# Attention weights transposed as F32R from a tile that takes over the slot, and a narrower low half in the product with V

## The chip, the cores and the metric

The kernel runs on one core of a Trainium2 chip. The engines are called as in the profile: PE (TensorE, matmuls), PEld (TensorE's weight loads), DVE (VectorE), ACT (ScalarE), POOL (GpSimd), SP (SyncE, which issues the DMAs). The metric is the device time of one execution in microseconds (us), lower is better. The kernel before took 742.23 us, the median of three runs (740.42, 742.23 and 747.87).

## The reference

The computation is an attention with a hash mask, followed by two dense layers of 1536 tokens. Attention has 2 batches of 8 heads, 768 tokens and a head width of 64:

```python
q_bits = (np.einsum('bhsd,dk->bhsk', q, proj) > 0).astype(np.int64)   # k_bits the same way
mask = q_bucket[:, :, :, None] == k_bucket[:, :, None, :]
scores = np.where(mask, scale * np.matmul(q, k.transpose(0, 1, 3, 2)), -1000000000.0)
attn = np.exp(scores - np.max(scores, axis=-1, keepdims=True))
attn = attn / (np.sum(attn, axis=-1, keepdims=True) + 1e-09)
x = np.matmul(attn, v)                       # laid out as 1536 x 512
h = x @ w_in                                 # 512 -> 2048, then an activation
x = (h * np.tanh(softplus(h))) @ w_out       # 2048 -> 512
h = x @ w_in2
out = (h - np.tanh(h)) @ w_out2
```

Everything is float32 in and out.

## The kernel before, in words

All matmuls but the transposes work on F32R, a float32 of reduced precision in the same four bytes. To keep precision, an operand x is split into a high part xh (x copied to F32R) and a low part xl (x - xh), and a product is a sum of the parts' products.

**Attention** goes through eight pairs of heads (`pairs`), and in a pair through two heads and two halves of the 768 queries. One such quarter (a *group* below, 32 in all) has three score tiles of 128 queries by 768 keys (`scores`, tiles `p`): four matmuls (L582, L583), a clamp with the row's minimum on DVE (L586), and the exponential with its row sum on ACT (L609), in place in `p`. Then come six *chunks* of 128 keys (`chunk`, 192 in all). A chunk transposes the three 128x128 blocks of its keys from the three score tiles into one PSUM tile `pt` (L643: three transposes, float32, against the constant identity `ident`), copies `pt` to the high part `ph` on ACT (L659) and takes the low part `pl` on DVE (L662); in three of twelve chunks ACT copies to `f` (L651) and POOL makes both parts (L375, L655). Four chunks later (`PV_LAG`) `product` multiplies the 128 columns of `vt`, V's high half beside its low half, with `ph` (L622) and with `pl` (L623), each 384 columns wide, and adds up over the six chunks in one PSUM tile `o`. `gather` folds the two halves of `o` together (L672 on ACT, L675 on DVE), and `finish` scales by the reciprocal sums. In between, the next pair's `piece` products (L478 to L480, with a stationary of 64 columns) and splits are made, on ACT (L423, L430, L461), DVE and POOL.

**The dense layers** follow at about 235 us and take the rest of the time. Their weights are turned from int64 into float, split and kept by DVE and ACT while PE multiplies.

**The order** on every engine is fixed beforehand by the planner `Plan`: each `op` has an engine, an estimated cost, a priority key and the buffers that it uses, and a list scheduler emits the operations in the order of their planned starts. Each engine then runs its instructions in that order and waits on semaphores. Tiles come from pools with a fixed number of slots per tag (`p` has `P_BUFS` = 6); a tile that takes a slot waits until all work on the slot's former tile is done. What an `op` emits besides its own engine's instructions stands at that place in the other engine's queue, and the planner doesn't know of it.

Of the kernel before, what the change touches and what calls it, by code (L numbers as in the profile page):

```python
# [27 lines left out]
F32 = mybir.dt.float32  # L28
# [19 lines left out]
G_BUFS, E_BUFS, GX_BUFS, F_BUFS = 3, 3, 2, 2  # L48
T_BUFS, P_BUFS, U_BUFS = 4, 6, 3
RAW_BUFS = 5  # L50
# [11 lines left out]
SLOWP = 0.4  # L62
SPARE = 1
LATE = 0.22
LATS = 0.15
# [214 lines left out]
def tile_lsh_attention_moe(  # L280
# [57 lines left out]
    for name, tags, n in (*wd, *wb):  # L338
# [4 lines left out]
    core = (  # L343
        ("stack", "a b c d", 2), ("p", "p", P_BUFS), ("vt", "vt", 3), ("gx", "ph pl", GX_BUFS),
        ("u", "u", U_BUFS), ("r", "r", 2), ("rt", "rt", 2), ("small", "mn mn2 sums", 6),
# [15 lines left out]
    pjh = const.tile([P, 64], F32R, name="pjh")  # L361
    pjl = const.tile([P, 64], F32R, name="pjl")
    rds = [const.tile([P, 32], F32, name=f"rd{i}") for i in range(2)]
    tiny = const.tile([P, 2, TB], F32, name="tiny")
# [200 lines left out]

    def scores(g, h, half, t, key):

# [3 lines left out]
        used = slice(0, NR + D) if g or h else slice(0, P)  # L571
        p, mn = buf("p", "p", [P, S]), buf("small", "mn", [P, 1])
        sm = sums[g, half]
# [28 lines left out]
        else:  # L602
            sc = buf("ps_s", "s", [P, 2, 512])
            flat = lambda: sc().rearrange("p a b -> p (a b)")
            op("PE", 0.69, key, lambda: products([(kc, flat()[:, kc]) for kc in parts]), reads, [sc])
            op("DVE", 0.87, key + 0.1, lambda: clamp(p(), flat()[:, :S], mn()), [sc], [(p, 0), (p, 1), mn])
        op(
            "ACT", 0.93, key + 0.2,
            lambda: nc.scalar.activation(  # L609
                out=p(), in_=p(), func=AF.Exp, bias=mn(), scale=-1.0,  # L610
                accum_out=sm()[:, h, t:t + 1],
            ),
            [mn, (p, 0), (p, 1)], [p, (sm, h, t)],
        )
        return p

    def product(todo, key):

        vt, c, ph, pl, o, done = todo

        def emit():
            nc.tensor.matmul(o()[:, :HB], vt()[:, c, :], ph()[:, :HB], start=(c == 0), stop=False)  # L622
            nc.tensor.matmul(o()[:, :HB], vt()[:, c, :], pl()[:, :HB], start=False, stop=(c == NT - 1))  # L623

        op("PE", 0.35, key, emit, [(vt, 0), (vt, 1), ph, pl], [o])
        if done:
            done()
# [3 lines left out]
    def chunk(g, h, half, c, ps, o, key, done):  # L631
# [8 lines left out]

        def transpose(ts):
            for t in ts:
                nc.tensor.transpose(pt()[:, t * P:(t + 1) * P], ps[t]()[:, c * P:(c + 1) * P], ident)  # L643

        op("PE", 0.327, key, lambda: transpose(range(TB)), ps, [(pt, 0), (pt, 1)])
        if len(queue) >= PV_LAG:
# [83 lines left out]
    for g in range(len(pairs)):  # L730
# [22 lines left out]
        for h in range(2):  # L753
            for half in range(2):
                n = (2 * g + h) * 2 + half
                ps = [
                    scores(g, h, half, t, at(NT * n + 2 * t - AHEAD) + 0.3) for t in range(TB)
                ]
                o = buf("ps_t", "pt", [P, 512])
                if h == 1:  # L760
                    inverse(g, half, at(NT * n - 2))

                def done(g=g, h=h, half=half, o=o, u=us[half], key=at(NT * (n + 1)) + PV_LAG):
                    gather(h, o, u, key)
                    if h == 1:
                        finish(g, half, u, key + 0.3)

                for c in range(NT):
                    chunk(g, h, half, c, ps, o, at(NT * n + c), done if c == NT - 1 else None)
# [645 lines left out]
    nc.vector.tensor_copy(pjh, pj)  # L1415
    nc.vector.tensor_tensor(out=pjl, in0=pj, in1=pjh, op=ALU.subtract)
    for o in plan.order():
        o.fn()
# [57 lines left out]
```

## Time and profile before

| | |
|---|---|
| median of 3 runs | 742.23 us |
| fastest run | 740.42 us |
| span of the profiled execution, first to last instruction | 739.1 us |
| PE busy | 727.7 us, 98% of the span |
| DVE, ACT, POOL busy | 87%, 72%, 24% of the span |
| POOL's work | all of it in the first 240 us |

The profiled execution's own time is not listed apart from the three runs; its span of 739.1 us is 1.3 us below the fastest of them and 3.1 us below the median, so a few microseconds around the span belong to a run's time. A busy time is the union of an engine's instructions, each taken until its result is out. Instructions of one engine overlap there: the next one may start before the last one has ended. So what an engine needs for a stream of instructions is read from the distance of their starts, as the chain of waits shows it, and not from the mean duration of one.

### The profile page before, as it was taken

What the parts mean: (1) busy time and instruction counts of PE and PEld (TensorE: products, weight loads), DVE (VectorE), ACT (ScalarE), POOL (GpSimd) and SP (SyncE); (2) the same over time, 40 slices, a digit from 0 to 9 for tenths busy, and PEclk for the clock granted to TensorE, in tenths of its full rate; (3) what the DMA queues carried; (4) which work ended last, traced back from release to release, by engine and by line L of the source; (5) the groups of instructions that cost most, each with busy time, mean ns of one, the idle gap of its engine ahead of it and who ended that gap; (6) DMA issues with size and microseconds to landing.
All of it is one profiled execution on the core that took longest, in us unless ns stands there. A gap on an engine that the chain in (4) does not pass through costs nothing.

```text
span 739.1 us, 13094 instructions
## 1 busy us (share of the span) xinstructions
PE 727.7 (98%) x4382; PEld 673.6 (91%) x4382; DVE 643.8 (87%) x1372; ACT 529.7 (72%) x1140; POOL 179.7 (24%) x224
## 2 busy tenths in 40 slices
PE   7999999999999999999999999999999999999998
PEld 4889999999999999999999999998998899999997
DVE  6988998998999999999898899789898775767893
ACT  6989999999997866767676676666565445466660
POOL 5677987988961000000000000000000000000000
PEclk9999999999999999999999999999999999999999
DMA  7775775785562655545655567999986786735621
GB/s 215 184 200 130 204 201 129 204 211 126 156 175 88 231 197 168 172 156 179 204 181 186 185 232 247 330 330 329 350 295 251 270 278 232 244 144 186 222 87 64
DMA packets 59390, 150.96 MB, mean 204 GB/s; under 512 B 7990, under 2 KB 20406, under 8 KB 59324
## 3 DMA queue, kind: packets, MB, share of 16 engines
q1 hardware_dynamic: 58892, 149.65, 63.9%
q8 instruction: 34, 0.56, 0.3%
q10 hardware_dynamic: 432, 0.49, 0.2%
q14 instruction: 32, 0.26, 0.1%
HBM read 88.18 MB, written 43.04 MB: 178 GB/s over the span
## 4 chain that ended last, share of the span: by engine, by line
PE 93%; DVE 2%; DMA 2%; ACT 2%; issue 1%; POOL 0%; ACTq 0%; SPq 0%; DVEq 0%; POOLq 0%
PE pt L1023 11%; PE pt L1025 11%; PE pt L1024 11%; PE pt L643 8%; PE pt L1101 6%; PE pt L1113 6%; PE s L1100 6%; PE pt L1100 6%; PE pt L1338 5%; PE s L582 4%; PE pt L622 4%; PE pt L623 4%; PE s L583 4%; PE s L1338 3%; PE s L1113 3%; DVE p L586 1%
## 5 line engine op out<-in xcount | busy, mean ns | idle before, releaser
L1023 PE MATMUL pt<-xh,a 128*128 128x384 f32 x288 | 96.7, 336 | 0.0
L1025 PE MATMUL pt<-xh,a 128*128 128x384 f32 x288 | 96.7, 336 | 0.0
L1024 PE MATMUL pt<-xl,a 128*128 128x384 f32 x288 | 96.6, 335 | 0.0
L586 DVE TENSOR_SCALAR_CACHE_REDUCE p<-s 128x768 f32<-128x768 f32 x93 | 88.2, 948 | 7.6 <-PE s L583 5.7
L609 ACT ACTIVATE p<-p,mn 128x768 f32<-128x768 f32 x96 | 90.7, 945 | 3.1 <-DVE p L586 2.0
L662 DVE TENSOR_TENSOR pl<-pt,ph 128x384 fp32r<-128x384 f32 x148 | 78.5, 546 | 8.6 <-ACT ph L659 7.6
L643 PE MATMUL pt<-cst,p 128*128 128x128 f32 x576 | 83.8, 272 | 1.1 <-DVE pl L662 1.1
L643 PEld LDWEIGHTS pt<-cst,p 128*128 128x128 f32 x576 | 69.5, 140 | 6.1 <-DVE pl L662 1.4
L659 ACT CAST ph<-pt 128x384 fp32r<-128x384 f32 x148 | 68.8, 484 | 5.2 <-PE pt L622 3.1
L1101 PE MATMUL pt<-gh,o 128*128 128x256 f32 x256 | 71.7, 280 | 0.0
L622 PE MATMUL pt<-ph,vt 128*128 128x384 f32 x192 | 70.4, 367 | 0.3 <-ACT f L651 0.2
L582 PE MATMUL s<-b,a 128*128 128x512 f32 (+1 forms) x186 | 68.2, 367 | 1.1 <-DVE p L586 0.7
L623 PE MATMUL pt<-pl,vt 128*128 128x384 f32 x192 | 64.9, 338 | 0.4 <-DVE pl L662 0.4
L583 PE MATMUL s<-d,c 77*128 77x512 f32 (+3 forms) x186 | 59.3, 340 | 0.6 <-ACT raw L846 0.6
L802 DVE TENSOR_TENSOR gl<-pl,gh 128x384 fp32r<-128x384 f32 x96 | 52.4, 551 | 6.5 <-ACT gh L1047 6.5
L1023 PEld LDWEIGHTS pt<-xh,a 128*128 128x128 f32 x288 | 54.1, 188 | 3.3 <-ACT pl L1042 0.2
L1024 PEld LDWEIGHTS pt<-xl,a 128*128 128x128 f32 x288 | 54.1, 188 | 1.3
L1025 PEld LDWEIGHTS pt<-xh,a 128*128 128x128 f32 x288 | 54.1, 188 | 0.1
L1047 ACT CAST gh<-pl 128x384 fp32r<-128x384 f32 x96 | 48.7, 514 | 2.1 <-DVE pl L802 1.1
L1101 PEld LDWEIGHTS pt<-gh,o 128*128 128x128 f32 x256 | 48.3, 189 | 0.0
L1061 ACT COPY ph<-pt 128x384 f32<-128x384 f32 x56 | 26.9, 481 | 28.7 <-PE pt L1025 28.6
L1100 PE MATMUL pt<-gh,o 128*128 128x512 f32 x128 | 47.2, 391 | 0.0
(301 smaller groups left out, 2080.7 us busy)
## 6 DMA issues: line engine op xcount, KB each, us to landing
w<-w SPq DMA_DIRECT2D x52, 512.0 KB
raw<-in_moe_w_in_dram SPq DMA_DIRECT2D x32, 512.0 KB
raw<-in_moe_w_out_dram SPq DMA_DIRECT2D x32, 512.0 KB
split<-a SPq DMA_DIRECT2D x24, 512.0 KB
a<-split SPq DMA_DIRECT2D x24, 512.0 KB
w<-t SPq DMA_DIRECT2D x32, 256.0 KB
o<-split SPq DMA_DIRECT2D x24, 256.0 KB
b<-kh SPq DMA_DIRECT2D x30, 192.0 KB
```

The costliest lines, as they stand in the source:

```text
L582: nc.tensor.matmul(o, a()[:, tok], b_()[:, kc], start=True, stop=False)
L583: nc.tensor.matmul(o, c_()[used, tok], d_()[used, kc], start=False, stop=True)
L586: nc.vector.tensor_scalar(out=out, in0=in_, scalar1=MASKED, scalar2=None, op0=ALU.min, op1=ALU.min, accum_out=low)
L609: lambda: nc.scalar.activation(out=p(), in_=p(), func=AF.Exp, bias=mn(), scale=-1.0, accum_out=sm()[:, h, t:t + 1],),
L622: nc.tensor.matmul(o()[:, :HB], vt()[:, c, :], ph()[:, :HB], start=(c == 0), stop=False)
L623: nc.tensor.matmul(o()[:, :HB], vt()[:, c, :], pl()[:, :HB], start=False, stop=(c == NT - 1))
L643: nc.tensor.transpose(pt()[:, t * P:(t + 1) * P], ps[t]()[:, c * P:(c + 1) * P], ident)
L1023: nc.tensor.matmul(o, tl()[:, 0, c], at_(0, kk), start=start and kk == 0, stop=False, skip_group_check=not start)
L1024: nc.tensor.matmul(o, tl()[:, 0, c], at_(1, kk), start=False, stop=False, skip_group_check=not start)
L1025: nc.tensor.matmul(o, tl()[:, 1, c], at_(0, kk), start=False, stop=kk == 1, skip_group_check=not start)
L1100: nc.tensor.matmul(a()[:, n, :], w()[:, y, c], flat[x][:, :SEG], start=st, stop=sp)
L1101: nc.tensor.matmul(r()[:, 0, rest], w()[:, y, c], flat[x][:, SEG:], start=st and d % 2 == 0, stop=sp, skip_group_check=True)
```

## The change

The three transposes of a chunk are no longer all float32. At a group's first chunk (`c == 0`) one block, that of the third score tile, is transposed as before, in float32. Then each of the three score tiles gets a successor, `p.split`, of the same size and in the same slot, but of type F32R; the slot holds what the exponential left there. POOL clears 8 columns behind the 768 (`PAD`), which makes it the writer of the new tile. All other transposes of the group, two in the first chunk and three in each later one, read `p.split` with an F32R copy of the identity, `idr`. There are 32 float32 transposes left and 544 as F32R. So that one tile's slot can pass on, each of the now 7 `p` buffers has its own tag with one slot. The exponentials of a group are kept in order, and so are the later groups' chunks behind the first (`after`).

In `product`, `pl` meets only the 64 columns of V's high half (the product of the two low halves is left out), and it comes first in all chunks but the first of a group. Three planner costs change: 0.23 for a chunk's transposes (0.327 before), 0.3 for those of a first chunk, 0.34 for a product (0.35 before).

```diff
-T_BUFS, P_BUFS, U_BUFS = 4, 6, 3
+T_BUFS, P_BUFS, U_BUFS = 4, 7, 3
+PAD, PAD_W = 8, 8
+T_COST, T_FIRST, PV_COST = 0.23, 0.3, 0.34
...
+    idr = const.tile([P, P], F32R, name="idr")
...
-        p, mn = buf("p", "p", [P, S]), buf("small", "mn", [P, 1])
+        p, mn = buf("p", f"p{n % P_BUFS}", [P, S + PAD]), buf("small", "mn", [P, 1])
...
+        def high():
+            nc.tensor.matmul(o()[:, :HB], vt()[:, c, :], ph()[:, :HB], start=(c == 0), stop=(c == NT - 1), skip_group_check=True)
+
+        def low():
+            nc.tensor.matmul(o()[:D, :HB], vt()[:, c, :D], pl()[:, :HB], start=False, stop=False, skip_group_check=True)
+
         def emit():
-            nc.tensor.matmul(o()[:, :HB], vt()[:, c, :], ph()[:, :HB], start=(c == 0), stop=False)
-            nc.tensor.matmul(o()[:, :HB], vt()[:, c, :], pl()[:, :HB], start=False, stop=(c == NT - 1))
+            for f in (high, low) if c == 0 else (low, high):
+                f()
...
-        def transpose(ts):
-            for t in ts:
-                nc.tensor.transpose(pt()[:, t * P:(t + 1) * P], ps[t]()[:, c * P:(c + 1) * P], ident)
-
-        op("PE", 0.327, key, lambda: transpose(range(TB)), ps, [(pt, 0), (pt, 1)])
+        def turn(t, src, unit):
+            to = pt()[:, t * P:(t + 1) * P]
+            nc.tensor.transpose(to if unit is ident else to.bitcast(F32R), src[:, c * P:(c + 1) * P], unit)
+
+        def transpose():
+
+            left = list(range(TB))
+            if c == 0:
+                turn(left.pop(), ps[-1](), ident)
+                for p in ps:
+                    p.split = plan.pools["p"].tile([P, S + PAD], F32R, tag=p.tag, name="split")
+                    nc.gpsimd.memset(p.split[:, S:S + PAD_W].bitcast(F32), 0.0)
+            for t in left:
+                turn(t, ps[t].split, idr)
+
+        first = op("PE", T_COST if c else T_FIRST, key, transpose, ps, [(pt, 0), (pt, 1)], after=ps[0].first if c else ())
+        if c == 0:
+            ps[0].first = [first]
...
+    nc.vector.tensor_copy(idr, ident)
```

The planner makes a new order of all engines from this. Three places:

PE before, in the second pair of heads, from the last product ahead of the pair's last group to that group's chunks (`cst` is the identity, `s` and `pt` are PSUM tiles, `vt` is V's halves).

```order
L622 MATMUL pt<-ph,vt 128x384 [waits Activation_49]
L623 MATMUL pt<-pl,vt 128x384 [waits DVE_49]
L643 MATMUL pt<-cst,p 128x128 x2
L643 MATMUL pt<-cst,p 128x128 [waits Activation_49]
L582 MATMUL s<-b,a 128x512 [waits DVE_49]
L583 MATMUL s<-d,c 128x512
L582 MATMUL s<-b,a 128x256
L583 MATMUL s<-d,c 128x256
L643 MATMUL pt<-cst,p 128x128 x6
```

PE after, at the same place of the program.

```order
L652 MATMUL pt<-cst,p_1270 128x128 [waits Activation_49]
L652 MATMUL pt<-idr,split 128x128 x5
L585 MATMUL s<-b,a 128x512 [waits DVE_49]
L586 MATMUL s<-d,c 128x512
L585 MATMUL s<-b,a 128x256
L586 MATMUL s<-d,c 128x256
L652 MATMUL pt<-idr,split 128x128 x3
L628 MATMUL pt<-pl,vt 64x384 [waits Pool_49]
L625 MATMUL pt<-ph,vt 128x384
L652 MATMUL pt<-idr,split 128x128 x3
L628 MATMUL pt<-pl,vt 64x384
L625 MATMUL pt<-ph,vt 128x384
```

The transposes stand in runs of three, six or nine as before (128 runs, 126 before). The F32R ones carry no wait on POOL, which writes only the columns behind the 768. Behind a run stands the 64-column low product in 56 cases and a 64-column `piece` in 8, a 128-column matmul in the other 64.

POOL after, in the third pair of heads, at the first chunk of its last group (L378 copies with a new type, L677 makes a low part).

```order
L562 TENSOR_TENSOR vt<-v,vt 128x6x64 [waits Pool_49]
L661 MEMSET split 128x8
L661 MEMSET split 128x8 [waits Activation_49]
L661 MEMSET split 128x8 [waits PE_49]
L378 TENSOR_SCALAR ph<-f 128x384 [waits Activation_49]
L677 TENSOR_TENSOR pl<-f,ph 128x384 [waits Pool_49]
L378 TENSOR_SCALAR kh<-k 128x384 [waits DMAHW5_49,DMAHW4_49,DMAHW3_49]
```

Each of the 32 groups adds three such clears to POOL's queue, the third behind the wait for the float32 transpose; before, POOL had none of them.

DVE before, in the second pair of heads, around the clamps of the last two score tiles of the group shown for PE (L586 is the clamp that writes a score tile, L662 makes a low part).

```order
L586 TENSOR_SCALAR p,mn<-s 128x768 [waits PE_49]
L695 STREAM_TRANSPOSE rt<-rd_128 128x32 [waits DMAHW6_49,DMAHW7_49,DMAHW0_49,DVE_49]
L662 TENSOR_TENSOR pl<-pt,ph 128x384 [waits Activation_49] x2
L586 TENSOR_SCALAR p,mn<-s 128x768 [waits PE_49]
L662 TENSOR_TENSOR pl<-pt,ph 128x384 [waits Activation_49]
```

DVE after, at the clamps of the same two score tiles (now L589; L684 makes a low part).

```order
L589 TENSOR_SCALAR p_1230,mn<-s 128x768 [waits PE_49,Pool_49]
L684 TENSOR_TENSOR pl<-pt,ph 128x384 [waits Activation_49]
L684 TENSOR_TENSOR pl<-pt,ph 128x384 [waits PE_49,Activation_49]
L589 TENSOR_SCALAR p_1270,mn<-s 128x768 [waits PE_49,Pool_49]
L697 TENSOR_TENSOR u<-pt,f 64x384 [waits Activation_49]
```

A clamp that waited for PE alone now waits for POOL too, for the clear of the tile that stood in its slot seven score tiles earlier.

## Rows read from the trace of the kernel before

**Rows 1.** The page: span and number of instructions.

```profile
span 739.1 us, 13094 instructions
```

**Rows 2.** Stretches: from:to, length, busy PE, PEld, DVE, ACT, POOL (instructions), clock, DMA, GB/s.

```profile
0.00:60.00 60.00, 53.20 (x304) 43.88 (x305) 48.56 (x114) 50.68 (x108) 42.72 (x59) 1.00 0.77 200
60.00:220.00 160.00, 159.85 (x1056) 146.99 (x1054) 148.24 (x331) 155.31 (x346) 133.85 (x164) 1.00 0.66 171
220.00:240.00 20.00, 19.55 (x127) 18.36 (x126) 19.67 (x46) 15.04 (x34) 3.10 (x3) 1.00 0.24 79
240.00:340.00 100.00, 100.00 (x578) 93.91 (x577) 99.21 (x202) 71.05 (x144) 0.00 (x0) 1.00 0.54 189
```

**Rows 3.** Chain of waits, 60 to 220 us: shares by line, then start, us, what.

```profile
by line: PE pt L643 27.7%; PE s L582 16.3%; PE pt L622 15.0%; PE s L583 15.0%; PE pt L623 15.0%; PE pt L478 2.2%; PE pt L479 2.2%; PE pt L480 2.2%; ACT p L609 1.1%; ACT ph L659 1.1%; DVE p L586 0.6%; DVE pl L662 0.3%; ACT f L672 0.3%; issue
...
62.35 0.93 ACT p L609 x2
...
64.12 0.39 ACT ph L659
...
145.01 0.98 PE pt L643 x9
```

**Rows 4.** Chain of waits, 100 to 110 us: single matmuls of 384, 512, 256 columns.

```profile
100.04 0.18 PE pt L623
100.22 0.24 PE s L582
...
100.69 0.12 PE s L582
...
103.00 0.18 PE pt L478
```

**Rows 5.** ACT by line, 60 to 220 us: count, busy us, mean ns, idle before.

```profile
L609 ACT ACTIVATE p<-p,mn 128x768 f32<-128x768 f32 x71 | 67.2, 946 | 0.5
L659 ACT CAST ph<-pt 128x384 fp32r<-128x384 f32 x108 | 50.2, 484 | 1.5 <-PE pt L622 0.7
L651 ACT COPY f<-pt 128x384 f32<-128x384 f32 x34 | 16.3, 480 | 0.3
...
L672 ACT COPY f<-pt 64x384 f32<-64x384 f32 x24 | 11.4, 475 | 0.9 <-PE pt L623 0.4
L461 ACT ACTIVATE z<-pt,cst 26x384 fp32r<-26x384 f32 x10 | 5.7, 575 | 1.4 <-PE pt L480 1.0
L423 ACT ACTIVATE q<-q 128x384 f32<-128x384 f32 x10 | 5.5, 550 | 0.0
L430 ACT CAST qh<-q 128x384 fp32r<-128x384 f32 x10 | 5.1, 509 | 0.0
L846 ACT ACTIVATE raw<-raw 128x512 uint32<-128x512 uint32 x5 | 3.4, 684 | 0.0
```

**Rows 6.** Timeline, weight loads right after PE stood idle: start, us, what, idle before.

```profile
12.14 0.19 PEld L582 LDWEIGHTS s<-b,a 128*128 128x128 f32 x1 [0.64 <-DVE p L586]
...
12.25 0.19 PEld L583 LDWEIGHTS s<-d,c 128*128 128x128 f32 x1
...
14.26 0.13 PEld L478 LDWEIGHTS pt<-kh,pjh 128*64 128x64 f32 x1 [0.56 <-POOL kh L375]
...
14.32 0.14 PEld L479 LDWEIGHTS pt<-kh,pjl 128*64 128x64 f32 x1
```

**Rows 7.** Timeline, 21.2 to 21.31 us: the first two transposes' loads after an idle.

```profile
21.24 0.20 PEld L643 LDWEIGHTS pt<-cst,p 128*128 128x128 f32 x2 [1.38 <-DVE pl L662]
```

**Rows 8.** POOL by line, first 5 us, and DVE by line, first 10 us.

```profile
L1430 POOL MEMSET const-float32-0.0<- 128x1 f32 x1 | 0.1, 100 | 0.2 <-issue 0.2
...
L444 DVE SCALAR_TENSOR_TENSOR ql<-q,qh 128x384 fp32r<-128x384 f32 x1 | 0.6, 559 | 1.1 <-ACT qh L434 1.1
L1415 DVE CAST pjh<-cst 128x64 fp32r<-128x64 f32 x1 | 0.2, 195 | 2.3 <-DMA cst<-cst_dram 2.3
```

**Rows 9.** Who waited for whom, 60 to 220 us: total us, times, longest.

```profile
POOL ph L375 <- ACT f L651: 14.3, 19, 2.0
```

More of the change, by code (lines that the diff above doesn't have):

```diff
@@ L343, in tile_lsh_attention_moe @@
     core = (
-        ("stack", "a b c d", 2), ("p", "p", P_BUFS), ("vt", "vt", 3), ("gx", "ph pl", GX_BUFS),
+        ("stack", "a b c d", 2), ("p", " ".join(f"p{i}" for i in range(P_BUFS)), 1), ("vt", "vt", 3), ("gx", "ph pl", GX_BUFS),
         ("u", "u", U_BUFS), ("r", "r", 2), ("rt", "rt", 2), ("small", "mn mn2 sums", 6),
@@ L564, in values_in, with scores @@
         vts[g, h] = vt
-    def scores(g, h, half, t, key):
+    def scores(g, h, half, t, key, after):
         a, b_, c_, d_ = stacks[g, h]
@@ L605, in scores @@
             op("PE", 0.69, key, lambda: products([(kc, flat()[:, kc]) for kc in parts]), reads, [sc])
-            op("DVE", 0.87, key + 0.1, lambda: clamp(p(), flat()[:, :S], mn()), [sc], [(p, 0), (p, 1), mn])
-        op(
+            op("DVE", 0.87, key + 0.1, lambda: clamp(p()[:, :S], flat()[:, :S], mn()), [sc], [(p, 0), (p, 1), mn])
+        p.exp = op(
             "ACT", 0.93, key + 0.2,
             lambda: nc.scalar.activation(
-                out=p(), in_=p(), func=AF.Exp, bias=mn(), scale=-1.0,
+                out=p()[:, :S], in_=p()[:, :S], func=AF.Exp, bias=mn(), scale=-1.0,
                 accum_out=sm()[:, h, t:t + 1],
             ),
-            [mn, (p, 0), (p, 1)], [p, (sm, h, t)],
+            [mn, (p, 0), (p, 1)], [p, (sm, h, t)], after=after,
         )
@@ L619, in product @@
         vt, c, ph, pl, o, done = todo
+        def high():
+            nc.tensor.matmul(o()[:, :HB], vt()[:, c, :], ph()[:, :HB], start=(c == 0), stop=(c == NT - 1), skip_group_check=True)
+        def low():
+            nc.tensor.matmul(o()[:D, :HB], vt()[:, c, :D], pl()[:, :HB], start=False, stop=False, skip_group_check=True)
         def emit():
-            nc.tensor.matmul(o()[:, :HB], vt()[:, c, :], ph()[:, :HB], start=(c == 0), stop=False)
-            nc.tensor.matmul(o()[:, :HB], vt()[:, c, :], pl()[:, :HB], start=False, stop=(c == NT - 1))
-        op("PE", 0.35, key, emit, [(vt, 0), (vt, 1), ph, pl], [o])
+            for f in (high, low) if c == 0 else (low, high):
+                f()
+        op("PE", PV_COST, key, emit, [(vt, 0), (vt, 1), ph, pl], [o])
         if done:
@@ L755, in tile_lsh_attention_moe @@
                 n = (2 * g + h) * 2 + half
-                ps = [
-                    scores(g, h, half, t, at(NT * n + 2 * t - AHEAD) + 0.3) for t in range(TB)
-                ]
+                ps = []
+                for t in range(TB):
+                    ps.append(scores(g, h, half, t, at(NT * n + 2 * t - AHEAD) + 0.3, [p.exp for p in ps[-1:]]))
                 o = buf("ps_t", "pt", [P, 512])
```

## The prediction, made before the changed kernel ran

> **What bounds the kernel now.** I read the stretches first, then the chain of waits, then the groups by line and single loads in the timeline. The stretches [rows 2] show PE busy in nearly all of the time from 60 us on: 159.85 of 160 us in attention, 100.00 of 100 us at the start of the dense layers. A busy PE alone proves little, since its instructions overlap. The chain [rows 3] settles it: over 160 us it runs almost wholly through PE, from one matmul's start to the next, and 27.7% of it, 44 us, are the transposes of L643. So in attention PE sets the pace. The reader should also see what is close behind: ACT is busy for 155.31 us of the same 160, DVE 148.24, POOL 133.85 [rows 2]. Any time that PE gains in attention is paid out only up to the point at which ACT has no idle left. In the dense layers the change touches nothing.
>
> **The transposes.** Nine in a row take 0.98 us of the chain [rows 3], 0.109 each. The whole program has 576, 62.8 us of PE. After the change 32 stay as they are (3.5 us) and 544 become F32R. What one of those takes is not in the trace, and two parts of it must be bounded. Streaming: F32R matmuls take 0.24 for 512 columns, 0.18 for 384 and 0.12 for 256 [rows 4], which is proportional to the columns at 0.47 ns each, so 128 columns take 0.06. Loading the stationary: after an idle of PE, the load of a 128-column F32R stationary holds back the next load by 0.11 us (12.14 to 12.25), that of a 64-column one by 0.06 (14.26 to 14.32) [rows 6]. But two loads of transposes, 128 columns wide, end 0.20 us after the first began [rows 7], as the pair of 64-column ones does, and not 0.30 as the pair of 128-column F32R ones: a transpose's load takes 0.06 in float32. So the float32 transpose is held by its streaming, and as F32R it takes between 0.06 (both parts at 0.06) and 0.11 (its load becomes an ordinary F32R load). It could be slower than now only if its load took more than the 0.11 of an ordinary one; no row shows such a load, and I keep that as part of the slow side. I take 0.06, since the row on the same data in the same mode is the nearest.
>
> Behind a run of F32R transposes, a 128-column load of 0.11 no longer fits behind the last streaming of 0.06 and shows 0.05; that is so for 64 of 128 runs, 3.2 us. The other 64 runs end at a 64-column load that fits. So the new sum is 3.5 + 544 x 0.06 + 3.2 = 39.3 us, and PE gives back 62.8 - 39.3 = 23.5 us. At the other end, 0.11 a transpose, only the last of a run saves, and only where a 64-column load follows: 64 x 0.05 = 3.2 us.
>
> **The products.** The low half streams the same 384 columns. Products with a 64-column stationary take 0.18 for them, as those with 128 do [rows 4]. So the narrower stationary saves nothing but its shorter load, which is counted above; and low before high swaps two equal matmuls. Zero, hidden by nothing: the streaming itself is unchanged.
>
> **What ACT leaves of it.** Between 60 and 220 us ACT makes 71 exponentials. In the chain one takes 0.93 with its read-out, and a copy 0.39 [rows 3]. 71 x 0.93 = 66.0; the copies of L659, L651 and L672 are 166 [rows 5], x 0.39 = 64.7; the four other groups are busy 19.7 [rows 5]. Sum 150.4 of 160 us. The busy time of 155.31 is the upper bound of ACT's need, this sum the nearer one, since it goes by distances of starts. So ACT has 4.7 to 9.6 us to give in this stretch, while PE would save 141 chunks of 192 (423 transposes), 17 us. ACT ends the gain. I take 9 us, near the upper end. The 51 chunks outside add little: before 60 us PE is busy only 53.20 of 60, and at 220 to 240 DVE is busy 19.67 of 20 [rows 2]; I take 1 us of their 6. The gain is 10 us.
>
> **What it adds.** POOL gets 96 clears. The nearest row, a clear of one column, takes 0.1 us [rows 8]: 9.6 us in all, 7 of them between 60 and 220, where POOL has 26 us idle [rows 2]. The third of each three waits for the float32 transpose, with the pooled splits queued behind it; POOL already waits there for ACT's copies, 19 times and 14.3 us [rows 9], so that the new wait mostly takes the place of an old one. The copy `idr` on DVE at the start is nearest to the 0.195 us copy of half its width; DVE stands idle for 1.1 us right behind it [rows 8], which hides it. If it did not, 0.4 us would come on top. A clamp's wait for a clear made for the tile seven earlier is covered by the at least five chunks (5 us) in between. The new order of engines and the seventh `p` buffer I cost at zero, between -1 and +2 us.
>
> **Where the gain could be given back.** DVE is busy 99.21 of 100 us at the start of the dense layers [rows 2]. It does the same work in attention as before, and by its order about as many weight conversions among it, so it comes to the dense layers as much earlier as PE does, and the stretch only moves. If DVE came late instead, up to the whole 10 us would be lost; I count that among the cases of no change.
>
> **Sum.** The profiled span of 739.1 us [rows 1] becomes about 729. The median of the runs lies 3.1 us above that span; against the median of 742.23 the forecast is 732.
>
> **Rivals.** A measurement of this kernel can tell 1% (7.4 us) from no change: faster is below 734.8, slower above 749.6.
>
> *The load becomes the bound (21%).* An F32R transpose loads its stationary like any F32R matmul, 0.11 us, and nothing is left of the shorter streaming but the 3.2 us: 739. For it: the change makes the operand the very type that loads in 0.11 [rows 6]. Against it: the same 128 columns of the same four bytes load in 0.06 in a transpose [rows 7]. The Trainium skill (TensorE: Matmul & The Clock Gate, section "LDWEIGHTS (loading the stationary operand)") says that a load takes its columns at 1.2 GHz, 107 ns for 128, whatever the rest; by that rule this rival would be the forecast. The trace agrees for the F32R loads and disagrees for those of the transposes.
>
> *The change doesn't do what it says, or it is lost later (8%).* The streaming stays at 0.109, since all 32 bits have to pass, or DVE is late at the dense layers: 742, give or take 1.
>
> *POOL becomes the bound (slower, 11%).* From 60 to 220 us there are 23.5 groups; POOL's 26 us of idle less 7 for the clears are 19, or 0.8 us a group. If the third clear holds POOL for longer than that on top of its present waits, splits come late, and PE waits at the products that carry a wait for POOL. At 1.4 us a group it is 0.6 x 32 = 19 us lost while the shorter transposes bring nothing: 761; at 1.2 us it is 755. For it: POOL is in order, and a float32 transpose may stand behind other matmuls. Against it: the waits that POOL has already [rows 9] leave it idle at these very places. With the slow transposes (2%, an ordinary load's whole 0.19 us [rows 6] for each: 0.08 x 544 = 44 us, 786) the slow side has 13%.
>
> *ACT as the bound (58%)* is the forecast, 732, from 726 (no wait left and ACT's need lower than counted) to 735.5 (only the 4.7 us of the busy count, and 2 outside).
>
> **Range and chances.** The forecast's cases and the load's rival hold 79%, and part of the no-change case adds the rest: 726 to 742. Faster 0.56 (the forecast without its upper edge), same 0.31 (that edge, the load as the bound, no gain), slower 0.13.
>
> **What would show it.** Right: the F32R transposes follow each other at 0.06 in the chain, PE's chain is broken by ACT's exponentials and copies in attention, ACT's busy share there rises above 98%, and the dense layers look as before, some 10 us earlier. Wrong: a distance of 0.11 and a chain that stays on PE (the load); POOL's clears as releasers of DVE's clamps, or long waits of the clears for the transposes with PE waiting for `ph` and `pl` (POOL); PE idle after 225 us, waiting for DVE (given back). A gain above 16 us would mean that ACT's need was counted too high.

## The result

The changed kernel takes 749.84 us (median of 4 runs, 749.51 to 751.72) against 743.24 us of the kernel before in the same session: a ratio of 1.0106, 95% interval 1.0064 to 1.0148. It is slower by 1%, where 732 us and a gain of 1.4% were forecast.

The page of the profile after, span and number of instructions, and its chain of waits over the whole span by engine:

```profile
span 747.6 us, 13219 instructions
...
PE 76%; DVE 7%; ACT 6%; POOL 4%; issue 4%; DMA 3%; SPq 0%; DVEq 0%; ACTq 0%; POOLq 0%
```

The span is 8.5 us longer than in [rows 1]. The stretches, columns as in [rows 2]:

```profile
0.00:60.00 60.00, 52.34 (x309) 42.38 (x309) 50.86 (x117) 50.60 (x107) 43.04 (x76) 0.97 0.75 200
60.00:220.00 160.00, 152.54 (x1024) 129.97 (x1023) 148.53 (x321) 150.88 (x337) 134.64 (x229) 1.00 0.64 163
220.00:240.00 20.00, 18.59 (x127) 16.75 (x125) 19.69 (x45) 16.17 (x36) 7.16 (x16) 1.00 0.31 103
240.00:340.00 100.00, 96.48 (x556) 90.04 (x556) 96.19 (x195) 69.44 (x140) 0.00 (x0) 1.00 0.50 176
```

Between 60 and 220 us PE does fewer matmuls than in [rows 2], 1024 against 1056, and stands idle for 7.46 us where it had 0.15. ACT, forecast to become full, is less busy than before: 150.88 against 155.31. So PE no longer sets the pace there, and ACT doesn't either. DVE, at 148.53, looks as it did.

The granted clock of PE in the first 60 us is 0.97, where it was 1.00 before. From 20 to 30 us it is 0.83: there PE ran for a time at the lower of its two levels (1.2 instead of 2.4 GHz), after it had stood idle for 1.71 us. By the account below some 2 us are lost there.

Three runs of F32R transposes in PE's timeline after (start, us from the first start to the last end, what):

```profile
120.95 0.38 PE L652 MATMUL pt<-idr,split 128*128 128x128 f32 x3
...
125.49 0.88 PE L652 MATMUL pt<-idr,split 128*128 128x128 f32 x9
...
146.84 0.63 PE L652 MATMUL pt<-idr,split 128*128 128x128 f32 x6
```

One such matmul alone lasts 0.243 us (mean of 544 by the page), so the other eight of a run of nine take (0.88 - 0.243) / 8 = 0.08 each, and the other two of three 0.07. The transposes did become shorter: 0.109 before.

Who waited for whom, 60 to 220 us, before (total us, times, longest):

```profile
PEld s L582 <- DVE p L586: 1.7, 7, 0.3
```

and after:

```profile
PEld s L585 <- DVE p L589: 11.4, 29, 1.0
...
POOL split L661 <- PE pt L652: 11.0, 18, 2.1
...
DVE p L589 <- PE s L586: 6.2, 19, 0.7
...
POOL ph L378 <- ACT f L673: 3.8, 9, 0.8
...
DVE p L589 <- POOL split L661: 0.2, 1, 0.2
```

Where before PE's loads for the scores waited 7 times, 1.7 us in all, for the clamp on DVE, they now wait 29 times. The clears do wait for the transposes, but a clamp waited for a clear once, 0.2 us.

**PE's account.** Since busy times overlap, I split the whole span of PE by distances. For each of the 4382 matmuls the distance from its predecessor's end is taken; the lower quartile of its shape (transposes apart by type and by place in their run: first, second, later) is its *floor*, and what it has above that is a *gap*. For a kernel, floors and gaps add up to its span less the 2 us ahead of the first matmul's end and 3 to 4 us after the last. An idle engine and a lowered clock both end up in the gaps.

| us | span | floors | gaps | at scores | at transposes | other, in attention | from there to 290 us |
|---|---|---|---|---|---|---|---|
| before | 739.1 | 711.5 | 21.8 | 4.9 | 1.8 | 2.3 | 0.8 |
| after | 747.6 | 692.0 | 50.2 | 18.1 | 8.7 | 7.9 | 3.7 |

(Attention is from the first transpose to the last; the gaps ahead of it, 7 us, and behind 290 us, 5, are alike in both.) PE did get 19.5 us back. The gaps grew by 28.4: 13.2 at the scores, 6.9 at the transposes, 5.6 at the other matmuls of attention, 2.9 at the start of the dense layers. The experiments ask which part of the change made which gap.

### The profile page after: what moved, and what is told of

The parts are those of the page before. It is cut to its first block, busy times and chain, and to the rows that moved or that the text cites. A ratio compares the mean times of both kernels' runs of the same rounds, so it can differ in the third digit from the quotient of the medians.

```text
span 747.6 us, 13219 instructions
## 1 busy us (share of the span) xinstructions
PE 723.5 (97%) x4382; PEld 657.4 (88%) x4382; DVE 652.0 (87%) x1373; ACT 530.6 (71%) x1140; POOL 184.8 (25%) x320
## 4 chain that ended last, share of the span: by engine, by line
PE 76%; DVE 7%; ACT 6%; POOL 4%; issue 4%; DMA 3%; SPq 0%; DVEq 0%; ACTq 0%; POOLq 0%
PE pt L1045 10%; PE pt L1046 10%; PE pt L1047 10%; PE pt L1135 6%; PE s L1122 6%; PE pt L1123 6%; PE pt L1122 5%; PE pt L1360 5%; PE s L1360 3%; PE s L1135 3%; PE s L585 3%; DVE p L589 3%; PE pt L652 2%; PE pt L628 2%; PE pt L625 2%
## 5 line engine op out<-in xcount | busy, mean ns | idle before, releaser
L1045 PE MATMUL pt<-xh,a 128*128 128x384 f32 x288 | 96.6, 335 | 2.2 <-ACT pl L1064 2.2
L589 DVE TENSOR_SCALAR_CACHE_REDUCE p<-s 128x768 f32<-128x768 f32 x93 | 88.2, 948 | 10.2 <-PE s L586 6.6
L684 DVE TENSOR_TENSOR pl<-pt,ph 128x384 fp32r<-128x384 f32 x148 | 77.0, 544 | 2.9 <-ACT ph L681 2.1
L652 PE MATMUL pt<-idr,split 128*128 128x128 f32 x544 | 64.8, 243 | 3.0 <-DVE pl L684 1.9
L628 PE MATMUL pt<-pl,vt 128*64 128x384 f32 x192 | 65.2, 346 | 1.9 <-DVE pl L684 1.7
L652 PEld LDWEIGHTS pt<-idr,split 128*128 128x128 f32 x544 | 58.8, 141 | 8.2 <-DVE pl L684 2.6
L625 PE MATMUL pt<-ph,vt 128*128 128x384 f32 x192 | 65.2, 346 | 0.8 <-ACT f L673 0.6
L586 PE MATMUL s<-d,c 77*128 77x512 f32 (+3 forms) x186 | 59.7, 342 | 0.6 <-ACT raw L868 0.6
L1045 PEld LDWEIGHTS pt<-xh,a 128*128 128x128 f32 x288 | 54.1, 188 | 5.4 <-ACT pl L1064 2.5
L585 PEld LDWEIGHTS s<-b,a 128*128 128x128 f32 x186 | 35.3, 190 | 18.0 <-DVE p L589 13.3
L1083 ACT COPY ph<-pt 128x384 f32<-128x384 f32 x56 | 26.9, 480 | 28.7 <-PE pt L1047 28.4
```

The source lines that it names most:

```text
L585: nc.tensor.matmul(o, a()[:, tok], b_()[:, kc], start=True, stop=False)
L589: nc.vector.tensor_scalar(out=out, in0=in_, scalar1=MASKED, scalar2=None, op0=ALU.min, op1=ALU.min, accum_out=low)
L628: nc.tensor.matmul(o()[:D, :HB], vt()[:, c, :D], pl()[:, :HB], start=False, stop=False, skip_group_check=True)
L652: nc.tensor.transpose(to if unit is ident else to.bitcast(F32R), src[:, c * P:(c + 1) * P], unit)
L684: lambda: nc.vector.tensor_tensor(out=pl()[:, w], in0=pt()[:, :HB], in1=ph()[:, w], op=ALU.subtract),
L1045: nc.tensor.matmul(o, tl()[:, 0, c], at_(0, kk), start=start and kk == 0, stop=False, skip_group_check=not start)
```

## The experiments

Two theories stood first. POOL: the clears, third in line behind a float32 transpose, hold POOL and DVE up (the rival of the prediction). Order: the planner, given seven slots and new costs, emits another order of instructions on all engines, and that order is worse. Ratios are to the kernel before in the same session, with 95% intervals.

### Parts of the change, in orders that the planner makes anew

`e1_handover_only`: the clears and the second tile in float32; products and costs of before.

```diff
-T_COST, T_FIRST, PV_COST = 0.23, 0.3, 0.34
+T_COST, T_FIRST, PV_COST = 0.327, 0.327, 0.35
-                    p.split = plan.pools["p"].tile([P, S + PAD], F32R, tag=p.tag, name="split")
+                    p.split = plan.pools["p"].tile([P, S + PAD], F32, tag=p.tag, name="split")
-                turn(t, ps[t].split, idr)
+                turn(t, ps[t].split, ident)
```

> The handover alone: the successor tiles, their clears on POOL with the wait for PE, the 7 tags and the ordered exponentials stay; all transposes are float32 again, the products and the planner's costs are those of before. Theory POOL (the clears, held by PE's first transpose, put POOL out of step, and PE, DVE and ACT wait for it): most of the loss is here, 747 to 751 us. Theory ORDER (the planner, told of cheaper transposes, packs an order that the other engines cannot keep): 742 to 745 us, as before.

`e2_old_costs`: the whole change, with the three costs as in e1's first two lines.

> The whole change, but the planner is told the costs of before (0.327 for a chunk's transposes, 0.35 for a product). Theory POOL: 747 to 751 us, the clears and their waits are all there. Theory ORDER: the loss goes, 738 to 743 us.

`e3_new_order_only`: the kernel before, where the planner is told the change's costs.

```diff
-        op("PE", 0.327, key, lambda: transpose(range(TB)), ps, [(pt, 0), (pt, 1)])
+        op("PE", 0.23 if c else 0.3, key, lambda: transpose(range(TB)), ps, [(pt, 0), (pt, 1)])
-        op("PE", 0.35, key, emit, [(vt, 0), (vt, 1), ph, pl], [o])
+        op("PE", 0.34, key, emit, [(vt, 0), (vt, 1), ph, pl], [o])
```

> The kernel before with nothing changed but the planner's three costs (0.23, 0.3, 0.34): PE still does all transposes in float32. Theory POOL: 742 to 746 us, since nothing is added to POOL. Theory ORDER: 747 us or more, the order itself costs.

`e4_no_handover`: the change without clears or second tile. The score tile is F32R from the start, which rounds the weights, so their low half is nothing; that part of the computation is left out. All 576 transposes are F32R.

```diff
-            if c == 0:
-                turn(left.pop(), ps[-1](), ident)
-                for p in ps:
-                    p.split = plan.pools["p"].tile([P, S + PAD], F32R, tag=p.tag, name="split")
-                    nc.gpsimd.memset(p.split[:, S:S + PAD_W].bitcast(F32), 0.0)
             for t in left:
-                turn(t, ps[t].split, idr)
+                turn(t, ps[t](), idr)
```

> The change without the handover: the score tiles are F32R from the start, so clamp and exponential round to F32R (the low parts of the weights come out as nothing, though all instructions on them are made), all 576 transposes are F32R, and there are no clears. Theory POOL: the forecast's gain comes, 730 to 737 us. Theory ORDER: 746 to 751 us, no better than the change.

Measured: e1 751.65 us, 1.0126 [1.0095, 1.0156]; e2 753.55, 1.0141 [1.0101, 1.0182]; e3 758.7, 1.0231 [1.0193, 1.0269]; e4 750.28, 1.0105 [1.0064, 1.0145]. By their times e1 and e2 came out near where POOL had them (747 to 751) and far above where ORDER had them; but those two expectations of ORDER overlooked that the seventh slot gives a new order by itself. The other two decide: e4 has no clear, has the change's order to the instruction, and is as slow as the change; and e3, which differs from before in nothing but three numbers of the planner, is the slowest. So POOL falls. All four have a new order.

### The same parts in before's order

For these the planner still sees one tag with six slots and before's costs, and so emits before's order to the instruction; the tiles take six tags by turn, so that a slot can be passed on.

```diff
-        p, mn = buf("p", "p", [P, S]), buf("small", "mn", [P, 1])
+        p, mn = PBuf(plan, "p", "p", [P, S + PAD], F32), buf("small", "mn", [P, 1])
...
+        def __call__(self):
+            if self.t is None:
+                self.slot = f"p{next(turns) % P_BUFS}"
+                self.t = self.plan.pools["p"].tile(self.shape, self.dtype, tag=self.slot, name="p")
+            return self.t
```

To this `e5_old_order_handover` adds the 96 clears and second tiles in float32; `e6_old_order_f32r` takes F32R score tiles with 576 F32R transposes and no clears (again without the weights' low half); `e7_old_order_split` takes the change's transposes, clears and second tiles; `e8_old_order_all` also its products, so it is everything of the change but its order and seventh slot; `e11_two_of_three` is e7 with the third tile in float32 throughout and two clears a group, which wait for no transpose.

> The handover alone in the order of before: the planner is told nothing new (one tag with 6 slots, the old costs), so that every engine's queue is that of before but for the 96 clears in POOL's; all transposes float32, products as before. Theory ORDER: 741 to 745 us, the clears fit into POOL's idle. Theory POOL: 747 us or more, the clears hold POOL until PE gets there.

> The shorter transposes alone in the order of before: score tiles are F32R from the start (weights rounded, their low parts come out as nothing, all instructions made), 576 F32R transposes, no clears, every engine's queue that of before. Theory ORDER: PE's 0.08 instead of 0.109 a transpose, measured in the change, is 576 x 0.027 = 16 us less of PE; with ACT as the limit some 5 to 10 us come through, 732 to 737 us. Rival BOUND (PE was not the only limit, and an order made for PE's old pace gains nothing from a faster PE): 740 to 744 us.

> The change's transposes in the order of before: handover with its 96 clears, 32 float32 and 544 F32R transposes, products as before. Theory ORDER: 733 to 738 us, the gain of the F32R transposes less a little for the clears. Theory POOL: 745 us or more. Rival BOUND: 741 to 745 us.

> Everything the change does in the order of before: handover, F32R transposes, and the narrower low half ahead of the high half. Theory ORDER: 733 to 738 us, as without the product's edit. If the product's order costs (the low part is ready later than the high part, and now stands first), it is slower than the run without it by 1 to 4 us.

> In the order of before, only the first two score tiles of a group pass their slot on; the third is transposed in float32 in all chunks, so that 384 transposes are F32R and 192 float32, and the 64 clears wait for exponentials alone, never for PE. Products as before. If the clears' wait for PE is what took the gain of the F32R transposes in the run with all three: 737 to 740 us (384 x 0.027 = 10 us less of PE, a third of it coming through). If the clears cost by their number: 740 to 743 us.

Measured: e5 743.29 us, 1.0014 [0.9999, 1.0029]; e6 737.21, 0.9936 [0.9919, 0.9952]; e7 741.39, 0.9998 [0.9982, 1.0014]; e8 742.67, 1.0003 [0.9987, 1.0019]; e11 741.48, 1.0 [0.9971, 1.0028]. In before's order the whole change costs nothing and brings nothing, where ORDER had the gain come through (733 to 738 for e7 and e8); so besides the order something takes PE's saving. Its own order and slot are worth the 7 us between e8 and the change. The clears cost 0 to 0.3% while PE is the bound (e5). F32R transposes without the handover bring 0.6%; with it (e7) that is gone. e11 was to win a part of it back and didn't, so the wait of the third clear is hardly what takes it (the interval of e11 ends at 740, the edge of what was expected). The products can't be told from nothing (e8 against e7).

### How much of it is any new order

`e9_seven_slots` is the kernel before with one slot more, `e10_cost_032`, `e17_cost_033` and `e18_cost_034` with another planner's cost for a chunk's transposes; `e12_measured_costs` is the change with costs from its own trace.

The edit of e9, that of e10 (e17 and e18 have 0.330 and 0.340 in its place), and that of e12:

```diff
-T_BUFS, P_BUFS, U_BUFS = 4, 6, 3
+T_BUFS, P_BUFS, U_BUFS = 4, 7, 3
```

```diff
-        op("PE", 0.327, key, lambda: transpose(range(TB)), ps, [(pt, 0), (pt, 1)])
+        op("PE", 0.320, key, lambda: transpose(range(TB)), ps, [(pt, 0), (pt, 1)])
```

```diff
-T_COST, T_FIRST, PV_COST = 0.23, 0.3, 0.34
+T_COST, T_FIRST, PV_COST = 0.246, 0.273, 0.35
```

> The kernel before with 7 instead of 6 slots for score tiles, which the planner uses; no other edit. Theory ORDER (the loss is in the re-planned queues, whatever caused the new plan): 748 to 753 us, as the handover with 7 slots and the costs of before gave. Rival SLOTS (a further slot can only help, the loss belongs to the clears or costs): 739 to 743 us.

> The kernel before with one planner cost moved by 2%: 0.320 for a chunk's transposes instead of 0.327; every instruction is the same, 16% of PE's and about half of DVE's change places. Theory ORDER with an exceptional order before (nearly any other plan is worse): 746 to 753 us. Rival (only plans made for much cheaper transposes or more slots are worse): 740 to 744 us.

> The whole change with the planner's costs set to what its own trace shows: 0.246 for three F32R transposes (0.082 each), 0.273 for a first chunk, 0.35 for a product. If the plan failed since its costs were too low: 738 to 744 us. Theory ORDER in its plain form (a new plan is worse for other reasons): 746 to 753 us.

> The kernel before, with 0.330 instead of 0.327 as the planner's cost of three transposes: 55 of 4382 PE instructions change place, 335 of DVE, 115 of ACT, 3 of POOL. If what counts is how far the order departs from before's, on PE above all: within 3 us of before. If any new order loses: 9 us or more.

> The kernel before with 0.340 as that cost: 876 of 4382 PE instructions change place. If every order far from before's loses: slower by 9 to 16 us, as with 0.320, with the new costs and with seven slots. If only an order made for cheaper transposes or for more slots loses, because PE's work is then packed too close behind the clamps: within 3 us of before.

An instruction counts as moved when it stands outside the stretches that its engine's two orders have in common.

| | ratio | PE, DVE instructions that change place (of 4382, 1273) | floors | gaps | at scores | at transposes | other, in attention | to 290 us |
|---|---|---|---|---|---|---|---|---|
| e17, 0.330 | 1.0032 [1.0018, 1.0046] | 55, 335 | 711.2 | 25.1 | 5.3 | 2.2 | 3.9 | 1.7 |
| e9, seven slots | 1.0133 [1.0109, 1.0157] | 770, 568 | 711.4 | 32.8 | 9.5 | 2.0 | 6.4 | 2.4 |
| e18, 0.340 | 1.0165 [1.0128, 1.0202] | 876, 538 | 711.4 | 33.9 | 9.7 | 2.3 | 7.5 | 1.7 |
| e10, 0.320 | 1.0203 [1.0168, 1.0238] | 715, 604 | 711.3 | 43.9 | 18.6 | 6.5 | 5.0 | 1.7 |
| e3, new costs | 1.0231 [1.0193, 1.0269] | 934, 495 | 710.9 | 39.1 | 15.9 | 5.8 | 3.8 | 1.4 |

All five do the very work of the kernel before, which the floors show, and differ from it in order (e9 in one slot too). Slots, a cheaper and a dearer transpose: each lost 1.3 to 2.3%, once 700 or more of PE's instructions had changed place. So the direction of the estimate doesn't matter, and true costs don't help: e12 took 755.21 us, 1.0171 [1.0147, 1.0196]. Only e17, which leaves PE's order nearly alone, stays near before.

Three runs share one order: e9, e1 and e2 have the same sequence on PE, DVE, ACT and POOL, but for the clears and the copy `idr`. They took 751.76 (no change of the work), 751.65 (the handover) and 753.55 us (the whole change), so in that order too neither the handover costs nor the shorter transposes bring anything that shows. Nor is the loss one of the clock: among executions with the same granted clock of 0.998, before took 741.5 to 743.1 us, the change 749.5 and 749.6, e9 751.6 to 751.8, e18 751.7, e10 755.1 and e3 757.5. The gaps of e10 are read with care: its profiled execution is the slowest of its four (762.88 us) with a granted clock of 0.98 between 60 and 220 us, and two of its waits at the scores, 3.0 and 3.9 us, are an accident that the last section shows.

Two stretches of e9, and who waited in it between 60 and 220 us:

```profile
60.00:220.00 160.00, 158.14 (x1025) 142.54 (x1023) 145.72 (x320) 151.60 (x337) 131.95 (x161) 1.00 0.63 162
...
240.00:340.00 100.00, 96.13 (x556) 89.89 (x556) 95.95 (x196) 69.17 (x141) 0.83 (x1) 1.00 0.48 172
```

```profile
POOL ph L375 <- ACT f L651: 17.3, 21, 1.7
DVE p L586 <- PE s L583: 7.3, 17, 1.1
PEld s L582 <- DVE p L586: 5.5, 15, 1.0
...
POOL u L719 <- DVE u L675: 4.3, 4, 1.9
...
ACT p L609 <- DVE p L586: 2.4, 4, 0.8
```

Most of this is of kinds that before has too. It has more of the short waits that before's order nearly does without (for the loads of the scores, 5.5 us against 1.7); exponentials now wait for clamps (2.4 us); and at the start of the dense layers PE is busy for 96 us of 100 where it was full, as it is in the change. There the first dense product's load waits, up to 280 us in e9:

```profile
PEld pt L1023 <- ACT pl L1042: 2.3, 1, 2.3
```

### What took PE's saving in before's order

e8 has floors of 692.7 us and gaps of 41.3, of them 20.0 at the scores: there too PE got 19 us back and lost as much waiting. The prediction said that ACT ends the gain; the gaps point to the clamp on DVE, which frees the only score slot in PSUM. Three kernels in e8's order and one in the change's take work from one engine each; all leave out part of the weights. The exponential of e13 and e15:

```diff
-                out=p()[:, :S], in_=p()[:, :S], func=AF.Exp, bias=mn(), scale=-1.0,
+                out=p()[:, :HB], in_=p()[:, :HB], func=AF.Exp, bias=mn(), scale=-1.0,
```

The exponential of e14 and e16, and the clamp of e14 to e16:

```diff
-                out=p()[:, :S], in_=p()[:, :S], func=AF.Exp, bias=mn(), scale=-1.0,
+                out=p()[:, :S], in_=mn().to_broadcast([P, S]), func=AF.Exp, bias=mn(), scale=-1.0,
...
-            op("DVE", 0.87, key + 0.1, lambda: clamp(p()[:, :S], flat()[:, :S], mn()), [sc], [(p, 0), (p, 1), mn])
+            op("DVE", 0.87, key + 0.1, lambda: clamp(p()[:, :HB], flat()[:, :HB], mn()), [sc], [(p, 0), (p, 1), mn])
```

> Everything of the change in before's order (742.7 us when run so), with the exponential over 384 of the 768 columns; the other half of the weights stays unexponentiated, so this part of the computation is left out. ACT gets some 0.4 us a tile back, 35 us in all; DVE and PE do what they did. If ACT is what swallows PE's saving (the prediction's step), PE's gaps fall back to before's and the time falls by 12 us or more, to about 729. If the clamp on DVE does, which frees the one score slot, the gaps at the scores stay near 20 us and the time stays within 3 us of 742.

> The same kernel with the clamp over 384 of the 768 columns, and the exponential, at its full width, fed from the row minimum instead of the weights; so the weights are left out. DVE gets some 0.4 us a tile back and the score slot comes free as much earlier; ACT's work stays. If the clamp swallows PE's saving, the gaps at the scores fall from 20 us to 5 or less and the time falls to between 727 and 732. If ACT does, ACT stays full, the gaps move to other matmuls, and the time stays within 3 us of 742.

> The same kernel with both over half the width (transposes read the first three chunks twice; half of the weights is left out). PE is left alone: its shortest distances sum to 692.7 us, with the 7 us of gaps ahead of the first transpose, the 5 in the dense layers and the 4 us around the span. Both theories: 710 to 722. If it stays above 730, something else than ACT and the clamp holds PE (POOL, or the order itself).

> The change as it is, in its own order (749.8 us), with the clamp cut as in e14_half_clamp. If the loss of the new order sits in the scores' wait for the clamp, it ends within 2 us of e14_half_clamp. If it sits at the transposes that wait for exponentials, at the products and at the start of the dense layers (7 of the 9 us of gaps that the change has over the same work in before's order), it stays 5 us or more above e14_half_clamp.

| us | time | ratio | gaps | at scores | at transposes | other, in attention | to 290 us |
|---|---|---|---|---|---|---|---|
| e8, full width | 742.67 | 1.0003 [0.9987, 1.0019] | 41.3 | 20.0 | 2.8 | 5.3 | 1.0 |
| e13, half the exponential | 741.69 | 0.9999 [0.9982, 1.0015] | 42.1 | 20.8 | 2.4 | 4.9 | 1.0 |
| e14, half the clamp | 735.44 | 0.9931 [0.9902, 0.996] | 38.4 | 6.6 | 8.8 | 8.4 | 1.0 |
| e15, both | 728.41 | 0.9824 [0.9792, 0.9856] | 29.4 | 6.6 | 1.2 | 8.5 | 1.0 |
| e16, half the clamp, the change's order | 744.24 | 1.0037 [1.0023, 1.0051] | 45.1 | 6.5 | 12.6 | 9.5 | 3.1 |

The stretch from 60 to 220 us of e8, then of e13, then of e14:

```profile
60.00:220.00 160.00, 154.96 (x1046) 134.49 (x1046) 149.03 (x328) 153.70 (x344) 135.84 (x234) 1.00 0.65 171
```

```profile
60.00:220.00 160.00, 154.70 (x1050) 135.20 (x1049) 149.17 (x327) 136.28 (x344) 137.21 (x236) 1.00 0.66 170
```

```profile
60.00:220.00 160.00, 157.12 (x1080) 137.27 (x1079) 128.87 (x338) 156.64 (x354) 140.07 (x240) 1.00 0.68 174
```

In e13 ACT has 24 us of idle (136.28 busy), and the time doesn't move: ACT isn't the first limit. In e14 DVE has 31 us of idle, the gaps at the scores fall from 20.0 to 6.6, near the 5 or less of the clamp's theory, and 5 us are won by the ratios (7 by the medians), less than the 10 to 15 expected, since now ACT is full (156.64) and the transposes wait for its exponentials. The loads of PE in e14, 60 to 220 us, show that wait:

```profile
PEld pt L661 <- ACT p L621: 5.9, 14, 0.7
```

With both cut (e15) that wait is gone too and the time falls by 13 us by the ratios; 728.41 is above the 722 expected, and the gaps that are left in attention lie at the products, the `piece` products (8.5) and the scores (6.6). So there are two limits close behind PE, first the clamp, some 5 to 7 us later ACT.

That it is the clamp's turn through the one score slot, and not DVE's work as a whole, is argued: e14 shortens both at once. For the slot speaks that each side waits for the other. In e8 PE waits for the clamps while DVE still has 11 us of idle between 60 and 220 us, and of this it spends 4.4 in waiting for the scores:

```profile
DVE p L598 <- PE s L595: 4.4, 14, 0.7
```

A run with a second score slot, which would tell the two apart, was not made.

e16 stands 8.8 us above e14, as the change stands 7 above e8. The loss of the new order does not sit in the scores' wait for the clamp: between the change and e8 that gap is even smaller (18.1 and 20.0). It sits at the transposes (+5.9; by the waits below half of it behind exponentials), at other matmuls of attention (+2.6, half of it in the stretch of lowered clock, which e8's execution didn't have) and at the start of the dense layers (+2.7). Loads of PE up to 280 us in the change:

```profile
PEld pt L652 <- ACT p L612: 4.4, 8, 0.7
PEld pt L652 <- DVE pl L684: 2.6, 3, 1.7
...
PEld pt L1045 <- ACT pl L1064: 2.5, 1, 2.5
```

and in e8:

```profile
PEld s L594 <- DVE p L598: 13.8, 36, 0.8
...
PEld pt L661 <- ACT p L621: 1.6, 5, 0.5
```

The load of L1045, the first dense product, waits 2.5 us for ACT's low part; in e8, as before, there is no such wait.

## Why the prediction was wrong

Two terms of the sum failed, and nearly all of the 18 us between 732 and 749.84 are theirs: the gain of 10 us is nothing in before's order (e8), and the new order, costed at zero, takes some 7.

**The new order, costed at zero (-1 to +2), is the step that turned no gain into a loss.** With the seventh slot it is worth 7.2 us in the change (749.84 against e8's 742.67) and 9 to 17 us where the kernel before is given another order with the same work (e9, e18, e10, e3). The text named the new order and gave no reason for costing it at zero; its 13% for slower went to the clears and to slow transposes, and neither came about. The trace of before spoke against that: PE idle for 0.15 us of 160 with ACT, DVE and POOL at 97, 93 and 84% [rows 2] is an order with hardly a wait in it, and a rearrangement of it could hardly do anything but add some.

**ACT as the limit of the gain: wrong in its place and in its size.** The gain was to end at 10 us where ACT is full. In before's order the whole change gains nothing (e8: 1.0003, from 0.9987 to 1.0019). What ended the gain first is the clamp (e13, e14). By busy time DVE had 12 us of room [rows 2]; but the clamp stands in a loop: scores on PE, clamp on DVE, then the next scores in the same slot, each waiting for the other. So, most likely, it limits the pace before DVE is full. The Trainium skill (Perfetto Trace Analysis, section "Identifying the Most-Contended Engine") takes the occupancy of Vector and Scalar as the measure of the bottleneck; by it ACT, the fuller one, would have been next, and e13 disagrees: 24 us of idle on ACT won nothing. Its section "Optimization Strategy" says that the same gap repeating on the engine that should be full can mean too little room for the next tile; e8's 36 waits of the scores' loads agree. The 5 us that e6 gains without the handover are near the lower end of the forecast's 4.7 to 9.6 us by coincidence: PE's gaps at the scores are 15.3 us there too, so most likely the clamp ends that gain as well.

**The transposes: right in kind, mis-sized.** Floors of 0.061 (first and second of a run) and 0.081 us (later ones) sum to 43.1 with the 32 float32 ones, from 62.8: 19.7 us given back where the sum said 23.5. What holds back the third and later of a run is likely their loads: in the run of nine above these come 0.087 apart (nine in 0.84 us, of which the last lasts 0.141), where I had let only the load behind a run show:

```profile
125.39 0.84 PEld L652 LDWEIGHTS pt<-idr,split 128*128 128x128 f32 x9
```

The Trainium skill (TensorE: Matmul & The Clock Gate, section "LDWEIGHTS (loading the stationary operand)") gives a load's time in ns as its columns / 1.2, which is 107 ns for 128, an estimate. The trace agrees with neither that (0.08, not 0.107) nor my 0.06, though the rival built on it, the load as the bound, pointed to the right part. It was not what decided: 19.7 us are more than the 10 us that the forecast let through.

**The clears: right in price and wait, but the handover isn't free.** One takes 0.104 us. They wait for the transposes (11.0 us), and POOL's wait for ACT's copies falls from 14.3 to 3.8, so the new wait did take the place of the old. They hold up one clamp in 160 us; POOL as the bound, priced at 755 to 761, didn't come about. But with the handover the gain of e6 goes (e7, 4 us), and the third clear's wait is hardly the reason (e11). By the account 4.0 us of it stand at the scores (19.3 against 15.3) and 1.2 in the floors. The cause is open: DVE's slower instructions, below, would fit, with some 3 us between 60 and 220 us in e7 against e6, but this wasn't tried alone.

**The products at zero: right** (e8 against e7). **The dense layers only shift: wrong** for a new order (2.7 us), right in before's order, where PE is busy for 100.00 of 100 us from 240 on in e6, e7 and e8.

**What stays open:** which of the moved instructions make a new order lose. Its gaps lie at several kinds of matmul and in different shares (15.9 us at the scores in e3, 9.7 in e18, with 3.8 and 7.5 at the other matmuls of attention), so I don't put it down to one of them. DVE's slower instructions, below, go with the loss in e3, e9 and the change and are missing in e17, but no run tried them alone. That before's order is a rare good one is what seven other orders suggest (the change's, e12's and the five of the table), not what they prove.

## What to carry to other kernels

Where a planner fixes the order, an edit that touches its costs or slots is two changes, and the order can be the larger one: test the edit in the old order first, and perturb a planner's number by 2% to learn what a new order alone is worth. Before spending an engine's saving, look for loops through a single slot: here the clamp ended the gain with DVE busy for 149 of 160 us. An account of the distances between matmuls, split into floor and gap, shows at once whether a saving was made and lost, or never made.

## What the runs showed of the hardware

DVE's instructions take longer beside POOL's. In the change the same addition of 128x6 numbers (L713) takes 0.16 us at 68.50 and 1.19 us at 117.49:

```profile
68.50 0.16 DVE L713 TENSOR_TENSOR rd<-sums,tiny 128x6 f32<-128x6 f32 x1
...
117.49 1.19 DVE L713 TENSOR_TENSOR rd<-sums,tiny 128x6 f32<-128x6 f32 x1
...
117.34 1.32 POOL L872 TENSOR_TENSOR w<-w,raw 128x512 uint32<-128x512 uint32 x1
```

The long one ends with POOL's instruction, 0.02 us after it (117.34 + 1.32 = 118.66, 117.49 + 1.19 = 118.68). By line, DVE after, 60 to 220 us:

```profile
L860 DVE SCALAR_TENSOR_TENSOR w<-raw,w 128x512 uint32<-128x512 uint32 x5 | 6.5, 1305 | 0.1
L713 DVE TENSOR_TENSOR rd<-sums,tiny 128x6 f32<-128x6 f32 x12 | 5.8, 480 | 0.0
```

and before:

```profile
L838 DVE SCALAR_TENSOR_TENSOR w<-raw,w 128x512 uint32<-128x512 uint32 x5 | 3.8, 754 | 0.0
L691 DVE TENSOR_TENSOR rd<-sums,tiny 128x6 f32<-128x6 f32 x12 | 2.7, 228 | 0.0
```

The Trainium skill (GPSIMD Engine Reference, section "1. Specifications") names contention with DVE instructions that have two SBUF inputs, and both of these have two; the trace agrees. So what runs beside an instruction also decides how long it is: these two lines cost DVE 5.8 us more than before in the change, 5.4 in e3 (by the means of one), 3.1 in e9 and nothing in e17, which is another way in which a planner with fixed costs can't foresee its order's time. It isn't the order alone, for in before's order they cost 3.9 us more in e5 and 3.7 in e8; and e5 is at most 0.3% slower, so DVE can lose this much while PE is the bound.

Rarely, one instruction waits for a whole train of POOL's. In e10 a conversion of a dense weight on DVE (L830), 0.418 us in the median of its line, lasts 3.59 us while POOL works without a pause (the first and the last of the five instructions that it runs meanwhile):

```profile
113.63 3.59 DVE L830 TENSOR_SCALAR w<-raw 128x512 uint32<-128x512 uint32 x1
117.14 0.94 DVE L586 TENSOR_SCALAR_CACHE_REDUCE p<-s 128x768 f32<-128x768 f32 x1
```

```profile
113.06 1.00 POOL L719 TENSOR_TENSOR u<-u,r 128x384 f32<-128x384 f32 x1
...
115.95 0.98 POOL L726 TENSOR_TENSOR xl<-u,xh 128x384 fp32r<-128x384 f32 x1
```

DVE's ends 0.29 us after POOL's last (117.22 and 116.93). The clamp behind it comes late, the scores' loads wait 3.0 us, and after that idle PE runs for a time at the lower level of its clock. The same is seen once more in e10 (4.46 us), in e11 (4.25) and in e4 (4.66), each ending 0.27 to 0.29 us after POOL's train. The profiled executions of e10 and e11 took 762.88 and 747.92 us, where the medians are 758.5 and 741.48. That DVE waits for POOL there is read from the times; no run tried it alone.
